# Feed-forward stage of a fused layer gradient in column blocks of 768 and 512 with one buffer of row tiles, and zero fills moved among the stages

## The chip, the cores and the metric

The kernel runs on one core of one Trainium2 chip. The metric is the device time of one launch in microseconds; the kernel before has a median of 601.91 us over three runs (601.8 to 602.16). Engines are named as in the profile: PE (matmul), DVE (vector), ACT (scalar), POOL and SP (here issuers of DMA above all). Queue q0 carries the DMAs that POOL issues, q1 those that SP issues; both run on the same 16 DMA engines.

## The reference, cut to what matters

One token goes through a conditioned layer: modulation of `c` by `w_mod`, attention of 32 heads over the last 4096 keys of a cache, and a gated feed-forward stage. The outputs are the layer's value and the gradient of every input for a given `grad_out`.

```python
mod = silu(c) @ w_mod                       # sa, ca, ga, sb, cb, gb
h = layernorm(x) * (1 + ca) + sa
x = x + ga * attention(h, k_cache[-4096:], v_cache[-4096:], wq, wo)
h = layernorm(x) * (1 + cb) + sb
g = h @ w_gate ; u = h @ w_up               # 1024 -> 3584
x = x + gb * ((sigmoid(g) * u) @ w_down)    # 3584 -> 1024
# and jax.vjp of all of it: 10 gradients
```

The gradients of the two caches are 65536 rows per head group, zero except for the last 4096. The kernel writes those zeros itself: 120 pieces of 1 MB (six of them 960 KB), called fills, which make up about half of the 246.54 MB that the DMA engines move.

## The kernel before, in words

The order of all work is written out by hand (`manual_schedule`): each engine runs its instructions in the order of the source. DMA goes mostly through POOL's queue: `zero(n)` pops and issues n fills there, `load_ug` (L942) loads row tiles of `w_up` and `w_gate`, and gradient tiles are stored there. SP's queue carries `w_down` (`load_wd`, L931), small pieces of `w_mod` and some stores at the end. A fill has no data to wait for. With `after=` it waits for a named instruction (`dep`), so that it starts at a chosen point of the computation, and it stands in POOL's order like everything else. A DMA on POOL's queue also waits until the one eight places ahead of it on that queue has landed.

The stage that the change rewrites treats the 3584 hidden columns in NB = 7 blocks of FB = 512. For a block q:

- `load_ug(q, j0, 4)` brings four of the eight row tiles j of `w_up` (k = 0) or `w_gate` (k = 1), 128 x 4 x 512, 512 KB each. The tiles have two buffers (`q % 2` in `ug_v`), so those of block q + 2 are loaded while block q + 1 is worked on.
- `front(q)` (L1030): 32 matmuls give h @ w_up and h @ w_gate of the block as rows in a PSUM bank (`fg`).
- `gates` (L1039 on): DVE turns the rows into columns (a multiply by a mask and a sum), ACT takes sigmoid, and writes zeros into the bank for the next block.
- `turned` (L1053, L1054): the first JT = 3 row tiles are transposed on PE and copied back by ACT, so that PE can do their part of dh2 in `turned_mm` (L1060). The other five are done by DVE.
- `wd_ttr` (L253 through `ttr`): four sums over rows of `w_down` times a broadcast gradient (`b1k`), which give dhh.
- `hh_ops`, `ffn_mm` (L1073): the hidden values and their product with `w_down`, 32 matmuls of one column. After each half, `load_wd` reloads the two rows of the tile just used for the next block: 512 KB on SP's queue.
- `dug_part` (L1088, L1090): the gradient of g and u is spread over 128 partitions by eight PE transposes; ACT copies one half out, DVE the other.
- Five `ttr` over the remaining row tiles (1024 elements each), in place, give DVE's part of dh2. The loads for block q + 2 and the fills `Z_FFN[q]` are issued between these.

`side(n)` puts n unrelated transposes of `wo` and `v` tiles (L916 on PE, L917 on ACT) between these steps: 46 of them, two at a time. They and `turned` share two PSUM banks. After the stage come the gradient stores: `dwd` (gradient of `w_down`: four outer products on DVE and one 1 MB store), `dw_rows` (gradient of `w_up` and `w_gate`: one 896 KB store per row tile), `dwo`, `sec`, `kv_store` and others, with fills `Z_HAND` and `Z_ROWS` between them. The last statement issues what fills are left.

The two statements that say most about the order in a block, of `turn` and of the loop over q:

```python
gates(); turned(q); side(2); wd_ttr(0); hh_ops(q); first = wd_ttr(1); ffn_mm(q, 0)
side(2); front(q + 1, range(4)); side(2); front(q + 1, range(4, KD))   # then the five ttr of block q
```

Of the kernel before, what the change touches and what calls it, by code (L numbers as in the profile page):

```python
# [22 lines left out]
FB = 512  # L23
NB = F // FB
# [32 lines left out]
Z_FFN = [(1, 0, 1)] + [(1, 1, 1)] * 4 + [(0, 2)]  # L57
Z_HAND = (1, 1, 2, 1, 1)
Z_ROWS = (1, 1, 1, 0, 1, 0, 1, 0)
JT = 3  # L60
JV = KD - JT
@with_exitstack
def kernel(
# [174 lines left out]
    def mulv(out, a, b):  # L238
        return tt(out, a, b, ALU.mult)
# [684 lines left out]
    ug_v = arena[:, 16 * KIB:48 * KIB].rearrange("p (h q j k f) -> p q h j k f", h=2, q=2, j=4, k=2)  # L924
    wd_v = ar(152, 8).rearrange("p (i d) -> p i d", i=4)

    def wd_dram(t, q):
        return t[q * FB:(q + 1) * FB, :].rearrange("(p i) d -> p i d", i=4)

    def load_wd(q, i0=0, n=4):  # L930
        nc.sync.dma_start(out=wd_v[:, i0:i0 + n, :], in_=wd_dram(B_w_down, q)[:, i0:i0 + n, :])  # L931

    def ug_part(view, q, j0, n):
        return view[:, j0:j0 + n, q * FB:(q + 1) * FB]

    def ug_tile(q, k, j0, n):
        return ug_v[:, q % 2, j0 // 4, j0 % 4:j0 % 4 + n, k, :]
# [26 lines left out]
    load_ug(0, 0, 4, (0,))  # L964
    fold_T[2]()
    bch(1)
    load_ug(0, 0, 4, (1,))
    fold_T[3]()
    bch(1)
    load_ug(0, 4, 4, (0,))  # L970
    bch(1)
    load_ug(0, 4, 4, (1,))
# [4 lines left out]
    load_wd(0, 0, 2)  # L977
# [3 lines left out]
    B_t[4] = scr  # L981
    mod_tiles(md_ps, sb_t, range(4, 8), False)
# [13 lines left out]
    load_ug(1, 0, 4)  # L996
    tr_unit(B_t[6], ar(60, 2))()
    load_wd(0, 2, 2)
# [4 lines left out]
    load_ug(1, 4, 4)  # L1003
# [11 lines left out]
    dug_b = scr  # L1015
    dug_b2 = dug_b.rearrange("p (k f) -> p k f", k=2)
    dh2acc = vt([P, NB * JV], "dh2acc")
    small = {k: vt([P, 4], k, dt) for k, dt in
             (("sg", FP32), ("om", FP32), ("dhh", FP32), ("hh_bf", BF16), ("hom", FP32))}
    hh_all = vt([P, 4 * NB], "hh_all")  # L1020
    dug_all = rows_all[:, 64:64 + 8 * NB]
    fg = new_bank("fg")
    nc.vector.memset(fg, 0.0)
    gu_ps, ffn_ps, dh2_ps = fg[:, 0:256], fg[:, 256:256 + KD], fg[:, 272:272 + JT]
    ffn = vt([P, KD], "ffn")
    gu_t = gb_rest
# [6 lines left out]
    def front(q, js=range(KD)):  # L1033
        for j in js:
            w = ug_v[:, q % 2, j // 4, j % 4, :, :].rearrange("p k (r i) -> p k i r", i=4)
            ffn_rows(gu_ps, h2_bf[:, j:j + 1], w, j == KD - 1)

    def gates():
        rows_to_cols(gu_t, gu_ps, 8, gu_ps)  # L1039
        nc.scalar.activation(out=small["sg"], in_=gu_t[:, 4:8], func=ACT.Sigmoid)  # L1040
        nc.scalar.activation(out=small["om"], in_=gu_t[:, 4:8], func=ACT.Sigmoid, scale=-1.0)
        nc.scalar.activation(out=gu_ps.rearrange("p (n d) -> p n d", n=2), func=ACT.Copy, scale=0.0,
                             in_=ident_f.rearrange("p (n d) -> p n d", n=1).broadcast_to([P, 2, P]))

    def ug_flat(q, j):
        return ug_v[:, q % 2, j // 4, j % 4, :, :].rearrange("p k f -> p (k f)")

    def turned(q):
        for j in range(JT):
            w, tp = ug_flat(q, j), new_tp("tp_ug")  # L1050
            for b in range(8):
                k, i = divmod(b, 4)
                nc.tensor.transpose(tp[:, b * P:(b + 1) * P], w[:, k * FB + i:k * FB + i + FB - 3:4], ident_bf[:, :])  # L1053
            nc.scalar.copy(out=w, in_=tp[:, :])  # L1054

    def turned_mm(q):
        for j in range(JT):
            w = ug_flat(q, j)
            for b in range(8):
                nc.tensor.matmul(dh2_ps[:, j:j + 1], lhsT=w[:, b * P:(b + 1) * P],  # L1060
                                 rhs=dug_all[:, 8 * q + b:8 * q + b + 1], start=False,
                                 stop=(q == NB - 1 and b == 7), skip_group_check=True)

    def hh_ops(q):
        hh, up = hh_all[:, 4 * q:4 * q + 4], gu_t[:, 0:4]
        mulv(small["hh_bf"], small["sg"], up)
        mulv(hh, small["sg"], up)
        mulv(small["hom"], hh, small["om"])

    def ffn_mm(q, i0):  # L1070
        for i in (i0, i0 + 1):
            for k in range(KD):
                nc.tensor.matmul(ffn_ps[:, k:k + 1], lhsT=wd_v[:, i, k * P:(k + 1) * P],  # L1073
                                 rhs=small["hh_bf"][:, i:i + 1], start=False,
                                 stop=(q == NB - 1 and i == 3), skip_group_check=True)

    def wd_ttr(*rows):
        for i in rows:
            last = ttr(scr, wd_v[:, i, :], b1k, small["dhh"][:, i:i + 1])
        return last  # L1080

    def dug_part(q):
        dug = dug_all[:, 8 * q:8 * q + 8]
        mulv(dug[:, 0:4], small["dhh"], small["sg"])
        mulv(dug[:, 4:8], small["dhh"], small["hom"])
        tp = new_tp("tp_dug")
        for i in range(8):
            nc.tensor.transpose(tp[:, i * P:(i + 1) * P], dug[:, i:i + 1].broadcast_to([P, P]), ident_bf[:, :])  # L1088
        o, v = dug_b.rearrange("p (k f i) -> p k f i", k=2, i=4), tp.rearrange("p (k i f) -> p k f i", k=2, i=4)
        nc.scalar.copy(out=o[:, 0, :, :], in_=v[:, 0, :, :])  # L1090
        return cp(o[:, 1, :, :], v[:, 1, :, :])

    dug_row = [ar(o, 7) for o in (24, 152)]
    def dug_rows(k):
        for q0 in range(0, NB, 2):
            n = min(2, NB - q0)
            tp = new_tp("tp_rows")
            for b in range(4 * n):
                c0 = 8 * (q0 + b // 4) + 4 * k + b % 4
                nc.tensor.transpose(tp[:, b * P:(b + 1) * P], dug_all[:, c0:c0 + 1].broadcast_to([P, P]), ident_bf[:, :])  # L1100
            nc.scalar.copy(out=dug_row[k][:, q0 * FB:(q0 + n) * FB].rearrange("p (s f j) -> p s f j", f=P, j=4),
                           in_=tp[:, 0:n * FB].rearrange("p (s j f) -> p s f j", f=P, j=4))

# [5 lines left out]
    def dwd(q, off, outer):  # L1109
        t = ar(off, 8).rearrange("p (i d) -> p i d", i=4)  # L1110
        for i in range(4):
            outer(t[:, i, :], hh_all[:, 4 * q + i:4 * q + i + 1], b1k)

        def store():
            nc.gpsimd.dma_start(out=wd_dram(out_8, q), in_=t)
        return store
# [7 lines left out]
    def turn(q, fills=0):  # L1124
        gates()
        turned(q)
        side(2)
        wd_ttr(0)
        hh_ops(q)
        first = wd_ttr(1)  # L1130
        ffn_mm(q, 0)
        if q + 1 < NB:
            load_wd(q + 1, 0, 2)
        zero(fills, wd_ttr(2, 3))
        ffn_mm(q, 2)
        if q + 1 < NB:
            load_wd(q + 1, 2, 2)
        last = dug_part(q)
        turned_mm(q)
        return first, last  # L1140

    rot[:] = [(psum, "mm"), (prq, "rq")]
    side(2)
    front(0)
    zero(Z_FOLD[2])
    zero(Z_FOLD[3], turn(0)[0])
    for q in range(NB):
        more = q + 1 < NB
        if more:
            side(2)  # L1150
            front(q + 1, range(4))
            side(2)
            front(q + 1, range(4, KD))
        else:
            side(len(jobs))
        for j in range(JT, KD):
            w = ug_flat(q, j)
            ttr(w, w, dug_b, dh2acc[:, q * JV + j - JT:q * JV + j - JT + 1])
            if j == 3:
                if q + 2 < NB:  # L1160
                    load_ug(q + 2, 0, 4, (0,))
                    zero(Z_FFN[q][0])
                    load_ug(q + 2, 0, 4, (1,))
                elif more:
                    zero(Z_FFN[q][1])
                    dwd(0, 24, outer_dve)()
                    zero(Z_HAND[0])
                else:
                    dwd(3, 16, outer_dve)()
                    zero(Z_HAND[3])  # L1170
        if q + 2 < NB:
            load_ug(q + 2, 4, 4, (0,))
            zero(Z_FFN[q][1])
            load_ug(q + 2, 4, 4, (1,))
            turn(q + 1, Z_FFN[q][2])
        elif more:
            dwd(1, 40, outer_dve)()
            zero(Z_HAND[1])
            turn(q + 1)
            dwd(2, 152, outer_dve)()  # L1180
            zero(Z_HAND[2])
            dug_rows(0)
    dwd(4, 32, outer_dve)()
    zero(Z_HAND[4])
# [16 lines left out]
    dx1b, m2 = layernorm_bwd_col(dln2, ln2, rstd2, "ln2b", lambda: dwd(5, 152, outer_dve)())  # L1201
# [6 lines left out]
    zero(Z_ROWS[0])  # L1208
    bcast(dattn_bf, KD, dattn_b, "V")
# [88 lines left out]
    for b in range(2):  # L1298
# [7 lines left out]
        for hh in range(4):  # L1306
            nc.tensor.matmul(dov[:, b, :, hh], lhsT=do_sb[:, hh * P:(hh + 1) * P], rhs=ident_bf[:, 0::32],
                             start=True, stop=True)
    for g in range(G):
        tr_unit(N_sb[:, g * 1024:(g + 1) * 1024])()  # L1310
    dwd(6, 32, outer_dve)()
    dw_rows(0, 2, 40, outer_dve)
    zero(Z_ROWS[1])
    dwo(2)
    dwo(0)
    do_bf = vt([P, HQ], "do_bf", BF16)
    cp(do_bf, do_ps)
    dwo(4)
# [178 lines left out]
```

## Time and profile before

| what | value |
|---|---|
| median of 3 runs | 601.91 us |
| time of the profiled execution | 602.02 us |
| its span, first to last instruction | 600.2 us |
| DMA moved | 246.54 MB, mean 411 GB/s; q0 93.8%, q1 9.5% of 16 engines' span |
| busy: PE, DVE, ACT, POOL | 415.4 (69%), 353.8 (59%), 247.5 (41%), 148.0 (25%) us |
| granted TensorE clock, mean | 0.808 |
| feed-forward stage, first `front` to the last block's sums | about 311.7 to 430 us of the span |
| packets under 8 KB | 18864 of 33645 |

Times in the trace count from the span's start. 1.8 us of the profiled execution lie outside its span. "DMA share" is the sum of the packets' own durations over 16 engines' time: it passes 1 where packets of two queues overlap on an engine, so the GB/s beside it say better whether the engines are at work.

### The profile page before, as it was taken

What the parts mean: (1) busy time and instruction counts of PE and PEld (TensorE: products, weight loads), DVE (VectorE), ACT (ScalarE), POOL (GpSimd) and SP (SyncE); (2) the same over time, 40 slices, a digit from 0 to 9 for tenths busy, and PEclk for the clock granted to TensorE, in tenths of its full rate; (3) what the DMA queues carried; (4) which work ended last, traced back from release to release, by engine and by line L of the source; (5) the groups of instructions that cost most, each with busy time, mean ns of one, the idle gap of its engine ahead of it and who ended that gap; (6) DMA issues with size and microseconds to landing.
All of it is one profiled execution on the core that took longest, in us unless ns stands there. A gap on an engine that the chain in (4) does not pass through costs nothing.

```text
span 600.2 us, 9825 instructions
## 1 busy us (share of the span) xinstructions
PE 415.4 (69%) x4004; PEld 246.7 (41%) x4004; DVE 353.8 (59%) x647; ACT 247.5 (41%) x398; POOL 148.0 (25%) x249
## 2 busy tenths in 40 slices
PE   3996789999999999979776477766652056364300
PEld 2784434334345455435455465555532045131000
DVE  3755499999510030194738488878877056876800
ACT  2489515558211024112246366665632057373200
POOL 3113113212222122222223033241335133241100
PEclk9998699999999999998988578787676557555555
DMA  8999999999999999999999999999999999999997
GB/s 349 421 418 423 411 457 406 430 424 438 433 420 391 453 433 393 461 425 412 387 417 417 347 355 408 409 409 421 424 425 425 429 396 425 423 425 419 419 415 235
DMA packets 33645, 246.54 MB, mean 411 GB/s; under 512 B 4781, under 2 KB 4781, under 8 KB 18864
## 3 DMA queue, kind: packets, MB, share of 16 engines
q0 software_dynamic: 28320, 225.98, 93.8%
q1 hardware_dynamic: 5232, 19.93, 9.5%
q8 instruction: 31, 0.51, 0.3%
q14 instruction: 14, 0.11, 0.1%
q10 hardware_dynamic: 48, 0.01, 0.0%
HBM read 78.13 MB, written 185.60 MB: 439 GB/s over the span
## 4 chain that ended last, share of the span: by engine, by line
PE 37%; DMA 21%; DVE 20%; ACT 8%; issue 7%; POOL 3%; ACTq 0%; POOLq 0%; DVEq 0%; SPq 0%
PE b_ps L773 17%; DMA out_dram<-arena 12%; DVE arena L236 6%; PE n_ps L716 6%; DMA arena<-in_B_w_down_dram 5%; DVE arena L249 4%; DVE arena L253 3%; ACT arena L527 2%; ACT arena L1281 2%; PE t_ps L674 2%; DMA out_dram<-zeros 2%; DVE scr L253 2%; DMA arena<-in_B_w_gate_dram 1%; PE tp_k L506 1%; PE tp_side L916 1%
## 5 line engine op out<-in xcount | busy, mean ns | idle before, releaser
L773 PE MATMUL b_ps<-arena 128*128 128x512 bf16 x512 | 118.6, 384 | 1.1 <-ACT arena L917 1.1
L917 ACT COPY arena<-tp_side 128x1024 bf16<-128x1024 bf16 x62 | 60.8, 1018 | 50.5 <-PE tp_side L916 50.3
L236 DVE TENSOR_TENSOR arena<-arena 128x2048 bf16<-128x2048 bf16 x64 | 76.5, 1223 | 2.3 <-PE n_ps L716 0.3
L773 PEld LDWEIGHTS <-arena 128*128 128x128 bf16 x512 | 49.3, 99 | 58.9 <-issue 5.8
L716 PE MATMUL n_ps<-arena 128*128 128x512 bf16 x256 | 65.6, 378 | 5.8 <-DVE arena L236 4.2
L203 POOL DMA_DIRECT2D out_dram<-out_dram x68 | 33.7, 496 | 116.8 <-PE n_ps L716 38.4
L916 PE MATMUL tp_side<-ident_bf,arena 128*128 128x128 bf16 x496 | 48.2, 262 | 12.7 <-DVE arena L236 4.7
L916 PEld LDWEIGHTS <-arena 128*128 128x128 bf16 x496 | 40.3, 120 | 22.1 <-issue 13.6
L249 DVE TENSOR_SCALAR arena<-arena,h 128x3584 bf16<-128x3584 bf16 (+1 forms) x24 | 28.6, 1192 | 32.1 <-DMA out_dram<-arena 32.1
L209 POOL DMA_DIRECT2D out_dram<-zeros x46 | 25.9, 566 | 67.6 <-DVE rows_all L236 23.0
L716 PEld LDWEIGHTS <-arena 128*128 128x128 bf16 x256 | 24.6, 97 | 41.2 <-issue 15.8
L253 DVE CUSTOM_DVE_ANT_0 arena<-arena,scr 128x1024 bf16<-128x1024 bf16 x35 | 40.8, 1220 | 0.2
L1277 PE MATMUL ps_kv<-arena 32*128 32x512 bf16 x64 | 24.2, 588 | 22.6 <-DVE arena L257 12.8
L253 DVE CUSTOM_DVE_ANT_0 scr<-arena,b1k 128x1024 bf16<-128x1024 bf16 x28 | 34.2, 1223 | 7.5 <-DMA arena<-in_B_w_down_dram 7.0
L1281 ACT ACTIVATE arena<-ps_kv 128x512 bf16<-128x512 f32 x48 | 25.4, 690 | 31.3 <-PE ps_kv L1277 31.1
L676 ACT CAST arena<-t_ps 128x512 bf16<-128x512 f32 x56 | 30.1, 589 | 12.1 <-PE t_ps L674 12.1
L245 DVE CAST arena<-b_ps 128x512 bf16<-128x512 f32 x6 | 4.2, 692 | 50.8 <-PE b_ps L773 50.8
L1053 PE MATMUL tp_ug<-ident_bf,arena 128*128 128x128 bf16 x168 | 14.4, 244 | 17.7 <-ACT arena L1054 17.7
L527 ACT COPY arena<-tp_wq 128x1024 bf16<-128x1024 bf16 x23 | 21.4, 1066 | 7.3 <-PE tp_wq L525 7.3
L1277 PEld LDWEIGHTS <-arena 32*128 32x128 bf16 x64 | 6.9, 117 | 38.7 <-issue 37.8
L1341 PE MATMUL dh_ps<-dattn_bf,arena 128*128 128x1 bf16 x48 | 2.1, 167 | 29.2 <-ACT arena L1337 29.2
L942 POOL DMA_DIRECT2D arena<-in_B_w_up_dram x14 | 10.7, 761 | 43.1 <-DVE dh2acc L253 22.7
(325 smaller groups left out, 686.8 us busy)
## 6 DMA issues: line engine op xcount, KB each, us to landing
out_dram<-zeros POOLq DMA_DIRECT2D x46, 1024.0 KB, 11.8
out_dram<-arena POOLq DMA_DIRECT2D x35, 1024.0 KB, 11.8
out_dram<-arena POOLq DMA_DIRECT2D x16, 896.0 KB, 11.5
arena<-in_A_wq_dram POOLq DMA_DIRECT2D x8, 1024.0 KB, 21.1
arena<-in_A_wo_dram POOLq DMA_DIRECT2D x8, 1024.0 KB, 12.5
arena<-in_w_mod_dram POOLq DMA_DIRECT2D x7, 1024.0 KB, 18.7
arena<-in_B_w_up_dram POOLq DMA_DIRECT2D x14, 512.0 KB, 9.4
arena<-in_B_w_gate_dram POOLq DMA_DIRECT2D x14, 512.0 KB, 13.3
```

Of the source, the lines that this page charges most:

```text
L203: ins = nc.gpsimd.dma_start(out=as_rows(region, BIGP).bitcast(FP32), in_=zero_src[:, 0:P * ZW // 4].rearrange("i (p x) -> (i p) x", p=BIGP ...
L236: return nc.vector.tensor_tensor(out=out, in0=a, in1=b, op=op)
L249: return nc.vector.tensor_scalar(out=out, in0=a, scalar1=s1, scalar2=None, op0=op0)
L253: return nc.vector.tensor_tensor_reduce(out=out, in0=w, in1=b, scale=1.0, scalar=0.0, op0=ALU.mult, op1=ALU.add, accum_out=acc)
L527: nc.scalar.copy(out=blk, in_=tp[:, :])
L676: nc.scalar.copy(out=o, in_=ps)
L716: mm = nc.tensor.matmul(nbank[k][:, :], lhsT=k_nat[:, g, t_ * DH:(t_ + 1) * DH], rhs=vp[:, t_ % 2, 4 * k:4 * k + 4, :].rearrange("p h d -> ...
L773: mm = nc.tensor.matmul(bbank[p][k][:, :], lhsT=a4[:, p, h, :], rhs=wo_t[u][:, a, k * 512:(k + 1) * 512], start=(i == 0 and a == 0), stop= ...
L916: nc.tensor.transpose(tp[:, i * P:(i + 1) * P], blk[:, i * P:(i + 1) * P], ident_bf[:, :])
L917: nc.scalar.copy(out=blk if dst is None else dst, in_=tp[:, :])
L1277: nc.tensor.matmul(ps[:, :], lhsT=rows[r, t8 * P:(t8 + 1) * P], rhs=bd[r, :], start=True, stop=True, tile_position=(32 * tc_, 0))
L1281: nc.scalar.activation(out=o, in_=v, func=ACT.Copy, scale=float(scale))
```

## The change

The blocks become five: `NI = (6, 6, 6, 6, 4)` groups of 128 columns, so four blocks of 768 columns and one of 512. There is one buffer of row tiles (24 KB instead of 32 KB per partition). A pair of row tiles of the next block is loaded as soon as this block has done with the old ones: j = 0, 1 after `turned_mm`, then 2 and 3, 4 and 5, 6 and 7 after their `ug_ttr`. A load is 128 x 2 x 768 (384 KB). JT falls from 3 to 2, so DVE does six tiles of 1536 elements instead of five of 1024.

The sums over the first n - 1 rows of `w_down` (`wd_ttr`) stand ahead of `gates` in DVE's order, only the last one behind. `w_down` comes as six row tiles, the first four in one 1 MB load, the other two in a 512 KB load. `dug_part` goes through two PSUM tiles and a buffer of its own (`dug_b`, no more `scr`). DVE's copy of the second half waits for PE there, where it waited for ACT.

Per block of the loop POOL issues one fill after `dug_part`, eight loads, and three fills behind the last pair (`Z_FFN = [(1, 0, 0, 3)] * 4`). The fills of the stage up to `Z_HAND` stay 22. `Z_ROWS` becomes eight ones (it had five), and the last statement finds none left, where it issued three. `dwd` stores come in parts of three rows (768 KB), nine in all instead of seven of 1 MB.

```diff
-FB = 512
-NB = F // FB
+NI = (6, 6, 6, 6, 4)
+NB = len(NI)
+I0 = [sum(NI[0:q]) for q in range(NB)]
+KF = F // P
...
-Z_FFN = [(1, 0, 1)] + [(1, 1, 1)] * 4 + [(0, 2)]
-Z_HAND = (1, 1, 2, 1, 1)
-Z_ROWS = (1, 1, 1, 0, 1, 0, 1, 0)
-JT = 3
+Z_FFN = [(1, 0, 0, 3)] * 4
+Z_HAND = (2, 2, 2)
+Z_ROWS = (1, 1, 1, 1, 1, 1, 1, 1)
+JT = 2
...
+    wd_off = [152, 154, 156, 158, 44, 46]
+    wd_row = [ar(o, 2) for o in wd_off]
+    dug_b = ar(40, 3)
...
+    def ug_off(q, j):
+        if NI[q] == 6:
+            return 16 + 3 * j
+        return 16 + 2 * j if j < 4 else 24 + 2 * j
...
-    load_ug(0, 0, 4, (0,))
+    load_ug(0, 0, 2, (0,))
...
-    load_ug(0, 4, 4, (0,))
+    load_ug(0, 6, 2, (0,))
...
-    load_ug(1, 0, 4)
+    load_ug(0, 2, 2)
...
-    load_ug(1, 4, 4)
+    load_ug(0, 4, 2)
...
     side(2)
-    front(0)
+    front(0, (0, 1, 6, 7))
+    turned(0)
     zero(Z_FOLD[2])
-    zero(Z_FOLD[3], turn(0)[0])
+    front(0, range(2, 6))
+    zero(Z_FOLD[3], wd_ttr(*range(NI[0] - 1)))
     for q in range(NB):
...
+        gates(q)
+        wd_ttr(n - 1)
+        side(1)
+        hh_ops(q)
+        dug_cols(q)
+        last = dug_part(q)
+        zero(z[0] if more else Z_HAND[0], last)
+        turned_mm(q)
+        if more:
+            load_ug(q + 1, 0, 2)
+        ffn_mm(q, range(4))
+        if more:
+            load_wd(q + 1, 0, 4)
+        ffn_mm(q, range(4, n))
+        if more and NI[q + 1] > 4:
+            load_wd(q + 1, 4, 2)
+        side(4)
...
+        ug_ttr(q, 2)
+        ug_ttr(q, 3)
+        if more and NI[q + 1] == 6:
+            load_ug(q + 1, 2, 2)
+            zero(z[1])
...
+        ug_ttr(q, 4)
+        ug_ttr(q, 5)
+        if more:
+            load_ug(q + 1, 4 if NI[q + 1] == 6 else 2, 2)
+            zero(z[2])
...
+        ug_ttr(q, 6)
+        ug_ttr(q, 7)
+        if more:
+            if NI[q + 1] == 6:
+                load_ug(q + 1, 6, 2)
+            else:
+                load_ug(q + 1, 4, 4)
+                dwd(24)
+            zero(z[3])
+            front(q + 1, (0, 1))
+            turned(q + 1)
+            side(2)
+            front(q + 1, (2, 3))
+            side(1)
+            front(q + 1, (4, 5))
+            side(1)
+            front(q + 1, (6, 7))
+            wd_ttr(*range(NI[q + 1] - 1))
```

The old `turn` and the old loop body are gone. In the rest of the diff `front`, `gates`, `turned`, `turned_mm`, `hh_ops`, `dug_rows` and `dwd` take the block's width, and five more `dwd` calls stand among the gradient stores.

## Prediction

> **What bounds the kernel now.** I read the page's slices first, then the windows over the feed-forward stage, then the chain and the DMA issues there.
>
> ```profile
> DMA  8999999999999999999999999999999999999997
> GB/s 349 421 418 423 411 457 406 430 424 438 433 420 391 453 433 393 461 425 412 387 417 417 347 355 408 409 409 421 424 425 425 429 396 425 423 425 419 419 415 235
> ```
>
> The DMA engines are the bound almost everywhere. No other engine passes 69% of the span. So an edit is worth what it adds to or takes from the time in which the 16 engines have nothing to move, plus any change in what moving costs. Two slices are low inside the span, 22 and 23 (330 to 360 us), and they lie in the stage that is rewritten. Its windows (columns: length, busy time of PE, PEld, DVE, ACT, POOL, clock, DMA share, GB/s):
>
> ```profile
> 326.00:337.00 11.00, 4.60 (x72) 3.46 (x61) 5.45 (x13) 6.41 (x10) 1.65 (x3) 0.78 1.10 410
> 337.00:350.00 13.00, 8.26 (x128) 6.33 (x129) 9.59 (x19) 4.49 (x5) 2.71 (x5) 0.66 0.87 290
> 364.00:378.00 14.00, 10.40 (x160) 8.35 (x160) 12.14 (x27) 9.90 (x13) 4.64 (x7) 0.76 1.10 403
> 394.00:410.00 16.00, 12.60 (x200) 9.74 (x193) 13.46 (x29) 9.71 (x13) 5.14 (x9) 0.80 1.14 410
> 410.00:430.00 20.00, 13.26 (x165) 11.96 (x163) 18.04 (x39) 13.78 (x18) 3.69 (x7) 0.66 1.12 424
> ```
>
> Full engines move 410 GB/s of the stage's mix and 424 of stores and fills alone. Six windows (311.7, 327.9, 349.5, 364.1, 378.5, 395 to 410.7, each from one `gates` to the next but the first) give 407, 336, 402, 405, 410, 411: over 99 us a mean of 391.6. Against 410 that is 99 x 18.4 / 410 = 4.4 us lost, nearly all at 337 to 350. Why, the chain says:
>
> ```profile
> 318.64 1.22 DVE scr L253
> 319.90 0.04 issue
> 319.94 18.48 DMA arena<-in_B_w_down_dram
> ...
> 341.31 1.05 PE tp_dug L1088 x8
> ...
> 343.05 0.70 DVE scr L245
> ```
>
> `w_down` of block 1, asked for at 319.07 and 319.94, came at 338.4; behind it stood POOL's next fill, issued at 341.35 (it waits for `dug_part`'s products), and the loads behind that. The queue ran dry at 337. From 350 on, two buffers of row tiles keep loads issued a block ahead: `gates` follow each other by 14.6 us (349.5, 364.1, 378.5), a block moves 6.29 MB = 15.3 us at 410, so the engines always have work.
>
> **What the change removes.** With another order that dry spell has no reason to recur as such: -4.4 us. What is late next is the question.
>
> **A block of 768 after the change.** It moves 4 fills (4.19 MB), row tiles 3.15 and `w_down` 1.57 MB: 8.91 MB, 21.7 us at 410. Its clock starts at DVE's `gates`, t. Rows: multiply plus sum 0.81 us (364.08 to 364.89) x 1.5 = 1.2; one row sum 1.15 (period in a run of `ttr`); five small products 0.6; so dug at t+3.0. PE's twelve transposes: eight took 0.62 to 1.05, so 1.2: t+4.2. DVE's copy 0.69 x 1.5 = 1.0: t+5.2, where the fill is issued, then the pair 0, 1, which also waits for `turned_mm` (24 in 0.8 us, t+5.0). `w_down` is issued after 32 more matmuls (1.0): t+6.0. At 341.35 a fill went into an empty queue and the rate stayed at 210 until 344: about 2.5 us to the stream; SP's should take 1 to 2.5. Bytes flow from t+7.
>
> DVE then does six sums of 1536: 1.147 x 1.5 = 1.7 each, to t+15.4, and issues follow them: pair 2, 3 at t+8.7, pair 4, 5 at t+12, pair 6, 7 with three fills behind it at t+15.4. Five sums over `w_down` (1.27 apart) end at t+21.8.
>
> The long chain is PE's. `front(q+1, (0, 1))` stands ahead of everything else and needs pair 0, 1. Ahead of that pair, or beside it, the engines move the fill (1.05 MB) and all of `w_down` (1.57): 3.41 MB with the pair, 8.3 us, so it lands at t+15.3 to 16.5; I take 15.6 for 16 engines that don't end together. Before, the same tiles had landed a block earlier. Behind it: `front` of two tiles 0.8 (16 matmuls of 256 took 1.08); `turned`, 0.5 and four ACT copies of 768 (1.02 x 0.75 = 0.8) through two PSUM banks, 3.7; the second unit of `side` 0.7; then three `front` of 0.8 and two `side` units of 0.7 to 1.0 between: 9.4 us, bounds 8.8 (all transposes 0.61 per eight) and 10.4 (all 1.01). The next `gates` come at t+25.0 (23.8 to 26.5), against t+21.8 for DVE and t+21.7 for the bytes. Three fills behind the last pair last 7.7 us and are gone when `gates` begin or soon after, and new bytes flow only at t+7: 3.3 us of dry queue per block.
>
> The row of 14.6 us beside that: x 1.5 is 21.9, so DVE alone would keep pace. The single buffer loses it.
>
> **The first block.** Its later pairs are issued where block 1's loads stood:
>
> ```profile
> arena<-in_B_w_up_dram POOLq DMA_DIRECT2D x1, 512.0 KB, 18.8
> arena<-in_B_w_gate_dram POOLq DMA_DIRECT2D x1, 512.0 KB, 15.9
> ```
>
> These two (window 302 to 307, issued at 302.13 and 306.38; last column: us to landing) land at 320.9 and 322.3. With 0.9 MB less ahead of the pair 4, 5 it lands near 320, and `gates(0)` go from 313.7 to t = 321. The queue: before, without what was issued at 324 to 329 (3.15 MB), it would have been empty at 337.5 - 7.7 = 329.8; now 1.05 MB fewer row tiles and 0.52 MB less `w_down` stand in it, 3.8 us: dry at 326.0, bytes again at 328: 2.0 us. Blocks 1, 2, 3 start at 346, 371, 396, with 3.3 us each. In block 3 the next block's tiles are smaller: 8.13 MB, 19.8 us, but its last loads wait for the sixth sum and land near t+20, `gates(4)` at t+22: 2.0 us, and 0.7 more until `Z_HAND`'s fills. Sum 2.0 + 9.9 + 2.0 + 0.7 = 14.6 us dry.
>
> [...] In the window 319 to 325 only q0 moves (113.2% share) although `w_down` had been asked for at 319; in 374 to 381 q1 has 43.9% beside q0's 66.3%. [...]
>
> **Small terms.** Row tiles come in packets of 3 KB per partition instead of 4, `w_down` in larger ones: blocks whose half is 4 KB packets run at 410 against 424, 0.5 us per 3.15 MB; a third more packets add 0 to 0.7 us over the 12.6 MB: +0.5. Seven turns become five and ACT copies fewer turned tiles, while DVE takes six tiles of eight: nothing either way, since DVE's 21.8 lies under the 25.0; without that cover it would be 0.1 us over the bytes' 21.7 per block. The three last fills move into `Z_ROWS`: the engines are full there (422 to 430), so the bytes only change places. At the end SP's queue alone moved 397 GB/s (568 to 573, q1 96.4%) against 424, and without POOL's three fills its last 3 MB run alone: +0.5. They may fill the dips at 480 to 500 (393, 417): 0 to -0.9, I take -0.4. Sum +0.6. `dwd` in nine parts: same bytes, 0.
>
> **The forecast.** On the profiled execution's 602.0 (1.8 of it outside the span): -4.4 + 14.6 + 0.6 = 612.8, and 0.1 less against the median 601.91: 612.7. A period of 24.5, nearer the chain's lower bound, gives 1.5 less; I set 612.0.
>
> **Rivals.**
> First, slower by less (0.22): `w_down` waits behind POOL's work, as at 319 to 325. Then pair 0, 1 lands after 1.84 MB, at t+12.2, PE is ready at t+21.6, and the last pair's landing decides, about t+22.7: 1.0 us dry per block. 2.0 + 3.0 + 2.0 + 0.7 = 7.7: 602.0 - 4.4 + 7.7 + 0.6 = 605.9. For it: 18.48 us of waiting in the chain. Against: in the later blocks `w_down` landed in about 10.
>
> Second, faster (0.24): the queue never runs dry, because sums ahead of `gates` and three fills behind the last pair cover the turn. It decides at a period of 21.7: if PE's chain behind pair 0, 1 were 6 us, or the pair landed by t+12 and the last `front` within 0.3 of the last pair. Price: 602.0 - 4.4 + 0.6 = 598.2, up to 601 with the first block's 2.0 and a little at each turn. For it: from 364 to 378 ACT is busy for 9.90 of 14 us and PE for 10.40, so both have room. Against: 8.3 us of bytes ahead of the pair.
>
> Third, slower still: all PE steps at the slow rate, period 26.0, 3 us more, 615.8. Row: the clock was 0.50 at 340 to 344, and eight transposes took 1.01 against 0.61. [...] I give it 0.12 beside 0.35 for the forecast's own period, and 0.02 to worse.
>
> That the order isn't as written is no rival: the built program has five sums ahead of the multiply on DVE and one and three fills around eight loads on POOL. No change within 0.2% (1.2 us, about what a measurement of this kernel can tell): 0.05, a dry time that happens to equal the old one.
>
> Faster 0.24, same 0.05, slower 0.71. The range of 8 in 10 reaches from the faster case, 598.0, to 617.0, the slow period with its first block late; the likeliest case alone is 607 to 617.
>
> **What would show it.** Right: `gates` 24 to 26 us apart; PE waiting for pair 0, 1 each time; GB/s dips of 3 us at each turn; the gradient stages unchanged at 420 to 430. Wrong: turns at 22 us, or 410 GB/s through 320 to 430.

## The result, and the profile after

The changed kernel takes 617.03 us (median of 4 runs, 615.8 to 617.65), the kernel before 601.86 in the same comparison: a ratio of 1.0258 (1.0228 to 1.0288). It is slower, as forecast, but by 15.2 us where the forecast of 612.0 said 10.1 (its sum, 612.7, said 10.8), and 0.03 us beyond the top of the range. The profiled execution took 615.8 us, its span is 613.8, 13.6 more than before. (Runs of the kernel before lie in two groups some 2 us apart, so below, differences under 2 us are not read from times alone.)

The slices of the page, where only 22 and 23 had been low:

```profile
DMA  9999999999999999999999997989999999999997
GB/s 352 421 417 422 414 462 403 400 459 428 392 455 426 431 427 421 415 437 412 427 395 374 341 316 274 376 295 316 424 424 411 424 427 423 425 425 426 424 419 306
```

Slices 21 to 27 (322 to 430 us) are now low, the whole feed-forward stage, and what follows is at 411 to 427 up to the last slice. The windows from each `gates` to the next (same columns as before the change; the last figure is GB/s, and the one ahead of it the DMA share, which passes 1 with one queue alone as well: 1.13 from 319 to 325 in the kernel before, where only q0 moved):

```profile
321.30:348.80 27.50, 17.37 (x214) 11.86 (x213) 19.90 (x32) 13.24 (x17) 8.63 (x13) 0.63 1.05 387
348.80:376.80 28.00, 16.48 (x214) 11.03 (x215) 19.92 (x32) 13.18 (x17) 7.96 (x12) 0.70 0.91 325
376.80:403.60 26.80, 16.70 (x214) 11.36 (x214) 19.93 (x32) 13.24 (x17) 7.88 (x12) 0.75 0.86 316
403.60:427.70 24.10, 14.78 (x207) 11.56 (x207) 18.82 (x32) 12.05 (x17) 7.87 (x12) 0.72 0.78 271
427.70:440.00 12.30, 8.81 (x126) 7.81 (x125) 11.33 (x27) 8.73 (x12) 3.54 (x7) 0.72 1.13 421
```

Against 410 GB/s that is 27.5 x 23 / 410 = 1.5 us lost in the first block, then 5.8, 6.1 and 8.2: 21.6 us, where the stage lost 4.4 before. No compute engine is near full in them (DVE 19.9 of 28.0, PE 16.5). So what ends each block is a wait. The chain through the first turn, from one block to the next (start, length, what; steps under 0.2 us are left out):

```profile
328.18 10.21 DMA arena<-in_B_w_gate_dram
338.44 1.19 PE fg L1040 x8
339.63 0.79 PE tp_ug L1071 x6
340.48 0.81 ACT arena L1072
341.33 0.77 PE tp_ug L1071 x6
342.18 0.41 ACT arena L1072
342.58 0.29 issue
342.87 0.81 ACT arena L1072
343.73 0.61 PE tp_side L918 x8
344.34 1.12 PE fg L1040 x8
345.45 0.55 PE tp_side L918 x8
346.01 1.12 PE fg L1040 x8
347.12 0.55 PE tp_side L918 x8
347.68 1.15 PE fg L1040 x8
348.85 0.58 DVE fg L238
```

This is the forecast's long chain, piece for piece: the gate half of pair 0, 1 asked for at 328.18 and in use at 338.44; two tiles of `front`; the turning, PE and ACT in turn; three more `front` with `side` units between; then `gates`. The block began at 321.27, so the period, the time from one block's `gates` to the next, is 27.6 us. The list of waits in that stage has one line for all turns, the first block's last pair and the last block's pairs among them (total, times, longest):

```profile
PE fg L1040 <- DMA arena<-in_B_w_gate_dram: 31.4, 6, 8.1
```

And the second turn seen from the DMA engines, in slices of 0.7 us from 349 to 377:

```profile
DMA  9940000059399999999999999999999999999999
GB/s 386 375 141 12 0 0 0 0 47 140 117 421 410 421 410 445 398 380 408 415 408 390 389 386 375 362 380 375 369 367 390 453 448 424 410 410 445 421 433 433
```

The last fill's bytes end at 351; the next block's first loads and fill are issued at 354.1, and the rate is full from 357 on: some 3.5 us of next to nothing and two of little. Where only row tiles move (364 to 370), the rate is 362 to 390, not 410.

The fourth block is another case. Its chain runs through DVE's sums to the last load, issued at 420.07 and landed 5.67 us later.

### The profile page after: what moved, and what is told of

It is laid out like the page before. It is cut to its first block, busy times and chain, and to the rows that moved or that the text cites. A ratio compares the mean times of both kernels' runs of the same rounds, so it can differ in the third digit from the quotient of the medians.

```text
span 613.8 us, 9435 instructions
## 1 busy us (share of the span) xinstructions
PE 413.4 (67%) x3803; PEld 236.4 (39%) x3828; DVE 359.3 (59%) x621; ACT 241.3 (39%) x390; POOL 155.4 (25%) x261
## 2 busy tenths in 40 slices
DMA packets 33517, 246.53 MB, mean 402 GB/s; under 512 B 4910, under 2 KB 5422, under 8 KB 18993
## 4 chain that ended last, share of the span: by engine, by line
PE 37%; DMA 24%; DVE 19%; issue 9%; ACT 6%; POOL 2%; ACTq 0%; DVEq 0%; POOLq 0%
PE b_ps L775 14%; DMA out_dram<-arena 13%; DMA arena<-in_B_w_gate_dram 8%; DVE arena L238 6%; PE n_ps L718 6%; DVE arena L251 5%; PE fg L1040 3%; DMA arena<-in_w_mod_dram 2%; DVE arena L255 2%; ACT arena L529 2%; PE t_ps L676 2%; PE w_ps L471 1%; ACT arena L1072 1%; PE tp_k L508 1%; PE tp_side L918 1%
## 5 line engine op out<-in xcount | busy, mean ns | idle before, releaser
L775 PE MATMUL b_ps<-arena 128*128 128x512 bf16 x494 | 114.3, 379 | 2.4 <-ACT arena L919 1.1
L775 PEld LDWEIGHTS <-arena 128*128 128x128 bf16 x512 | 48.7, 98 | 57.5 <-issue 3.4
L255 DVE CUSTOM_DVE_ANT_0 arena<-arena 128x1536 bf16<-128x1536 bf16 (+1 forms) x38 | 57.5, 1558 | 0.7
L918 PE MATMUL tp_side<-ident_bf,arena 128*128 128x128 bf16 x496 | 47.6, 258 | 11.4 <-DVE arena L238 6.2
L211 POOL DMA_DIRECT2D out_dram<-zeros x46 | 26.2, 572 | 101.3 <-DVE arena L247 57.1
L918 PEld LDWEIGHTS <-arena 128*128 128x128 bf16 x496 | 39.4, 118 | 29.1 <-issue 18.8
L1317 PE MATMUL ps_kv<-arena 32*128 32x512 bf16 x64 | 24.4, 588 | 28.8 <-DVE arena L259 15.8
L1040 PE MATMUL fg<-arena,h_bf 128*32 128x384 bf16 (+1 forms) x160 | 21.3, 623 | 31.5 <-DMA arena<-in_B_w_gate_dram 31.4
L718 PEld LDWEIGHTS <-arena 128*128 128x128 bf16 x256 | 24.6, 97 | 41.3 <-issue 15.8
L1321 ACT ACTIVATE arena<-ps_kv 128x512 bf16<-128x512 f32 x48 | 25.4, 698 | 37.5 <-PE ps_kv L1317 37.3
L1072 ACT COPY arena<-tp_ug 128x768 bf16<-128x768 bf16 (+1 forms) x20 | 14.1, 762 | 31.4 <-PE tp_ug L1071 31.3
L953 POOL DMA_DIRECT2D arena<-in_B_w_up_dram x19 | 13.9, 730 | 31.1 <-DVE dh2acc L255 23.0
```

Source lines behind the costliest of these rows:

```text
L255: return nc.vector.tensor_tensor_reduce(out=out, in0=w, in1=b, scale=1.0, scalar=0.0, op0=ALU.mult, op1=ALU.add, accum_out=acc)
L718: mm = nc.tensor.matmul(nbank[k][:, :], lhsT=k_nat[:, g, t_ * DH:(t_ + 1) * DH], rhs=vp[:, t_ % 2, 4 * k:4 * k + 4, :].rearrange("p h d -> ...
L775: mm = nc.tensor.matmul(bbank[p][k][:, :], lhsT=a4[:, p, h, :], rhs=wo_t[u][:, a, k * 512:(k + 1) * 512], start=(i == 0 and a == 0), stop= ...
L918: nc.tensor.transpose(tp[:, i * P:(i + 1) * P], blk[:, i * P:(i + 1) * P], ident_bf[:, :])
L1040: nc.tensor.matmul(out[32 * a:32 * a + 32, :], lhsT=col.broadcast_to([P, 32]), rhs=w[..., 32 * a:32 * a + 32], start=False, stop=stop, til ...
L1317: nc.tensor.matmul(ps[:, :], lhsT=rows[r, t8 * P:(t8 + 1) * P], rhs=bd[r, :], start=True, stop=True, tile_position=(32 * tc_, 0))
```

## The experiments

All but those named as the kernel before are the changed kernel with one edit, or with the edits that are named. Differences are against its 617.03 us; t is the start of a block's `gates`, as in the prediction.

**The first fill behind the first pair.** In the block's body, `zero(z[0])` goes from ahead of `turned_mm(q)` to behind the first load:

```diff
-        zero(z[0] if more else Z_HAND[0], last)
         turned_mm(q)
         if more:
             load_ug(q + 1, 0, 2)
+        zero(z[0] if more else Z_HAND[0], last)
```

> The changed kernel with one edit: a block's first fill of 1 MB goes into POOL's queue behind the gate and up loads of the next block's first two row tiles, no longer ahead of them. Bytes and work are unchanged. Theory (the turn from one block to the next waits for that pair of row tiles, which comes behind the fill and next to 1.5 MB of w_down, and the matmul chain of some 10.3 us runs only behind it): the pair lands some 2.5 us earlier, the periods between gates go from 27.6, 28.0, 26.8 to about 25, so about 609 to 610. Rival (only the sum of the bytes in the queue counts, so what stands first in it changes nothing): 616 to 617.5.

607.43 us (606.98 to 608.02), 9.6 less; ratio to before 1.012 (1.0089 to 1.015). It is more than was expected, because the pair came 3.5 to 4.2 us earlier and not 2.5: it landed at t+13.6, 13.6 and 13.0 instead of 17.1, 17.8 and 16.5, and the periods went from 27.6, 28.0, 26.8 to 24.3, 25.4, 24.3. The same bytes in another order: the theory holds, the rival (only their sum counts) does not. What is late next is the last pair, by the chain of that run:

```profile
335.14 1.67 DVE arena L255
337.12 0.71 POOL arena L953
337.83 6.35 DMA arena<-in_B_w_gate_dram
344.31 1.22 PE fg L1040 x8
345.56 0.58 DVE fg L238
```

DVE's sums release the last loads at 337.1, the second of them lands 6.35 us behind its issue, and one `front` stands behind it.

**`w_down` held back.** Its two loads depend on the first sum over the row tiles:

```diff
-        if more:
-            load_wd(q + 1, 0, 4)
...
-        ug_ttr(q, 2)
+        first = ug_ttr(q, 2)
+        if more:
+            dep(load_wd(q + 1, 0, 4), first)
```

> The changed kernel with one edit: the next block's w_down (1 MB and 512 KB) is issued only when the first of VectorE's six sums over the row tiles is done, so that it doesn't share the DMA engines with the first fill and the first pair of row tiles. Theory (as told for the fill put behind): 1.5 MB less in front of the first pair, which takes 3.5 us off it; the pair lands at about 13 to 14 us behind the gates instead of 17, the periods are about 24 to 25, so about 606 to 609. Rival (w_down takes the pair's place as the last that the next block waits for, or the bytes count in whatever order): the last pair or w_down's last rows end a period of 27 to 28, 615 to 618.

613.44 us (612.27 to 614.16), 3.6 less. `w_down` was issued only 0.9 to 1.7 us later (t+7.3 instead of 5.8 in the first block), so the edit did less than meant: the pair landed at t+15.6, 15.6 and 15.3, not 13 to 14, and the chain behind it took 11.4 and 11.5 us at the first two turns instead of 10.4 and 10.2 (sixteen `side` transposes 1.87 us instead of 1.31; the granted clock was 0.62 over each of these two blocks, 0.63 and 0.70 in the changed kernel). In kind it agrees with the theory; its number was missed.

**The chain made short.** `front(q + 1, range(KD))`, then `turned(q + 1)`, with all eight `side` units where four stood, ahead of PE's wait for the pair.

> The changed kernel with one edit: the next block's eight row tiles go through the forward matmuls in order, and the turning of the first two row tiles, with the side units between, stands behind them and ahead of nothing that loads (the side units stand in front of the loads instead). Theory (period = landing of the first pair + the chain of matmuls, copies and side units behind it, 10.3 us): the chain behind the first pair shrinks to about 4.6 us, but the last pair lands 6.3 us behind the first, so that 1 to 1.2 us of matmuls behind the last pair end the period: about 24.5 to 26, so about 608 to 612. Rival (the DMA queue alone ends the period, because its dry stretch is set by when the loads may be issued): the time stays at 616 to 618.

614.18 us (613.44 to 616.03), 2.9 less, with periods 24.4, 27.0, 26.1 and 26.2. Neither number came. The first turn did what the theory said (24.4); the others paid elsewhere (two stretches of that run's chain):

```profile
347.75 0.66 ACT arena L1072
348.50 0.65 issue
349.15 0.21 ACT sg L1055
...
363.62 7.78 DMA arena<-in_B_w_gate_dram
371.54 1.19 PE fg L1040 x8
```

ACT's copies of the turned tiles now stand ahead of the sigmoid that the products of `gates` need. The block's first fill is issued at t+6.9 and 7.0 instead of 5.2 and 5.6, and the last pair, which now ends the period, is late by that.

**The fills of the last stage as before.** `Z_ROWS = (1, 1, 1, 0, 1, 0, 1, 0)`.

> The changed kernel with one edit: the fills of the last stage are placed as before the change (three of the eight slots are empty and their fills come at the very end). Theory (spreading the fills costs nothing and brings nothing where the DMA engines are busy anyhow; the loss is in the feed-forward blocks): 616 to 618. Rival (the fills put in earlier push back stores that the end waits for, which is where the time beyond the forecast went): about 612.

619.93 us (618.77 to 622.19), 2.9 more, with `gates` at the same times as in the changed kernel to 0.5 us. Neither side had this: spreading the fills is a gain, and it hid part of the loss in the blocks.

**A fill in the dry time.** `Z_FFN = [(1, 0, 0, 4)] * 3 + [(1, 0, 0, 3)]`, `Z_HAND = (1, 1, 1)`.

> The changed kernel with one more 1 MB fill behind the last pair of row tiles in each of the first three blocks (Z_FFN's last number 4 in place of 3), taken from the hand-over behind the last block (Z_HAND 1, 1, 1 in place of 2, 2, 2). Theory (the time lost is DMA engines that stand idle at each turn, from the end of the fills 3 us behind the gates to the first new bytes at about 7 us, while the next block can't load before its predecessor's sums are done): a fill of 2.45 us fits into the idle 4 us and delays nothing, so gates come at the same times as in the changed kernel, with 3 MB more done: 7.3 us less, 609 to 611. Rival (the queue is not idle but waits on something that the fill only prolongs, so that each turn comes later by about as much as the fill takes): 616 to 618.

612.63 us (611.29 to 614.56), 4.4 less where 7.3 were expected. The hand-over, with three fills fewer, ran at 347 GB/s from 429.7 to 440 instead of 421: 10.3 x 74 / 421 = 1.8 us. And the second period was 29.5 instead of 28.0, so `gates(4)` came 2.0 us later. It is not shown that the fill did this. The pair landed only 0.3 us later (t+18.1), while the chain behind it took 11.4 us instead of 10.2, with the granted clock at 0.50 from 366.5 to 371; and the last run below, whose blocks are those of the changed kernel without any fill added, had the same second period (29.6). The dry time is real; a fill put in it is worth its 2.45 us (in the changed kernel, fills behind each other landed 2.4 us apart, at 375.3, 377.7 and 380.1) less what it leaves empty elsewhere.

**Both.** The fill behind the pair, `Z_FFN = [(1, 0, 0, 4)] * 2 + [(1, 0, 0, 5), (1, 0, 1, 3)]`, `Z_HAND = (1, 1, 1)`, `Z_ROWS = (0, 0, 1, 1, 1, 1, 1, 1)`.

> The changed kernel with the first fill of a block behind the first pair of row tiles, and five more fills in the blocks: Z_FFN (1,0,0,4), (1,0,0,4), (1,0,0,5), (1,0,1,3), taken from the hand-over (Z_HAND 1, 1, 1) and from the first two slots of the stage behind it. With the fill put behind alone it was 607.4, and its windows between gates moved 377, 367, 362 and 313 GB/s. Theory (idle DMA engines are the loss, and both remedies add up as far as idle time is left): some 2 us for each of the first two turns, 3 at the third and 1 to 1.5 in the fourth block, so 598 to 601, below the kernel before. Rival (with the fill put behind, the last pair ends the period, so every further fill ahead of the next block's loads delays the turn by its own 2.4 us): 606 to 609.

602.82 us (601.61 to 605.37, 10 runs), ratio to before 1.0038 (1.0019 to 1.0056). Its windows:

```profile
321.50:345.80 24.30, 17.80 (x214) 12.30 (x214) 19.93 (x32) 13.23 (x17) 9.23 (x14) 0.62 1.09 385
345.80:372.20 26.40, 16.45 (x215) 10.88 (x216) 19.95 (x33) 13.16 (x17) 8.54 (x13) 0.74 1.14 402
372.20:397.00 24.80, 16.22 (x214) 10.85 (x213) 19.92 (x32) 13.22 (x17) 9.88 (x15) 0.79 1.15 393
397.00:423.00 26.00, 15.13 (x206) 11.71 (x207) 18.81 (x32) 12.02 (x17) 7.69 (x12) 0.71 1.11 413
423.00:440.00 17.00, 11.01 (x148) 9.33 (x146) 14.77 (x33) 12.10 (x17) 3.40 (x6) 0.70 1.00 376
```

The four blocks lose 1.5, 0.5, 1.0 and nothing. `gates(4)` come only 4.7 us earlier than in the changed kernel, but 14.2 us are back: most of them from work done in time that had been idle. What kept it from the 598 to 601 expected is the emptied places: 376 GB/s at the hand-over in the last row, and 412 from 440 to 520, where the changed kernel had 422.

**The kernel before, its dry spell filled.** `Z_FOLD = (1, 1, 1, 0)`, first entry of `Z_FFN` `(1, 2, 1)`.

> The kernel before with its own dry stretch filled: two fills go from ahead of the gates of the first block (Z_FOLD's last number 0 in place of 2) into its second half (Z_FFN's first entry (1, 2, 1) in place of (1, 0, 1)), so that POOL's queue holds work while the DMA engines stand idle behind the second block's w_down; same bytes. Theory (the 4.4 us that the kernel before loses in this stage are one dry stretch, and any transfer put there is worth its length): the stage loses up to 4.4 us less, 597 to 599. Rival (the two fills only swap places with the loads they now stand ahead of, so that the next gates come later and the dry stretch moves on): 600.5 to 602.

598.85 us (598.3 to 600.17), ratio 0.9973 (0.9957 to 0.999). The third `gates` came at 343.7 instead of 349.5, and 328 to 344 moved 413 GB/s. As the theory said.

**The kernel before, with the last stage's fills spread and nothing else.** `Z_ROWS` all 1.

> The kernel before with only the last part of the change: one fill in each of the eight slots of the last stage, none left for the very end (Z_ROWS all 1). In the changed kernel, undoing this cost 2.9 us. Theory (without fills between them, the last stores don't keep the DMA engines full; that depends on how far the engines are behind the last work, and the kernel before is ahead by some 15 us of queue): the kernel before has no such loss, its last 40 us moved 423 and 409 to 425 GB/s, so 601 to 602. Rival (the spread fills are worth the same in both kernels): 598.5 to 599.5.

594.11 us (594.06 to 597.01), ratio 0.99 (0.9867 to 0.9933); its profiled span is 595.2, 5.0 below. More than even the rival had. Of the 5.0, 3.0 lie behind the last landing: it came 4.3 us ahead of the end before and 1.3 here. The other 2.0 are earlier bytes, 480 to 520 at 424 GB/s instead of 414 among them.

**Columns read in order.** In `front`, `(k r i) -> p k i r` becomes `(k i r) -> p k i r`.

> The changed kernel with one edit: the forward matmuls over w_gate and w_up read 32 neighbouring columns at a time, no longer every sixth one. It leaves out the right assignment of columns to rows, so what it computes behind that is not the reference's; loads, bytes and the number of matmuls are the same. Theory (a matmul of 384 columns took 0.14 us, one of 256 columns 0.067 us at the same granted clock, because the price goes by the stretch of memory that is stepped over, 12 bytes a step in place of 8): the eight of two row tiles take 0.8 us or less in place of 1.19, the chain behind the first pair goes from 10.3 to 8.7 us, the periods from 27.5 to about 26, so 612 to 613. Rival (the price goes by the columns or by the number of matmuls): they stay at 1.19 us, and the time at 616 to 618.

612.04 us (610.9 to 613.12), 5.0 less, as the theory had it. The matmuls (PE's timeline), first and second pair of a block and one pair of the last block, which has 256 columns, and below them two lines of the changed kernel:

```profile
338.40 0.83 PE L1040 MATMUL fg<-arena,h_bf 128*32 128x384 bf16 x8 [7.42 <-DMA arena<-in_B_w_gate_dram]
...
343.91 0.51 PE L1040 MATMUL fg<-arena,h_bf 128*32 128x384 bf16 x8
...
422.53 0.40 PE L1040 MATMUL fg<-arena,h_bf 128*32 128x256 bf16 x8 [1.39 <-DMA arena<-in_B_w_gate_dram]
```

```profile
344.27 1.19 PE L1040 MATMUL fg<-arena,h_bf 128*32 128x384 bf16 x8
...
425.88 0.62 PE L1040 MATMUL fg<-arena,h_bf 128*32 128x256 bf16 x8 [1.14 <-DMA arena<-in_B_w_gate_dram]
```

In order, 0.83 us at a granted clock of 0.50 and 0.51 at 1.00; with 12 bytes a step 1.19 at either (0.50 at 338.4, 1.00 at 344.3); with 8 bytes a step, for two thirds of the columns, 0.63 at 0.50 (at 418.6) and 0.62 at 1.00, against 0.40 in order at 1.00. The chain behind the pair took 8.1 us at the first turn and 9.6 at the second, for 10.4 and 10.2. So the step is the price of `front`.

**TensorE kept busy.** 64 transposes of `ident_bf` behind `side(4)`.

> The changed kernel with 64 more transposes of a constant tile on TensorE in each of the first four blocks, behind the side units and ahead of the wait for the next block's first pair, where TensorE idles 7 to 8 us; nobody reads them. Theory (the chain behind the pair is slow by the granted clock, 0.5 for most of each wait: six transposes took 0.79 us, sixteen of a side unit 1.87 or 1.31): with the clock kept up the chain takes 8.8 to 9.3 us in place of 10.3, and the time falls by 3 to 4.5 us, 612.5 to 614. Rival (the chain is copies and matmuls whose price the clock doesn't move, 1.19 us for the eight forward matmuls at 0.5 and at 1.0 alike): 616 to 618, or later by up to 3 us a turn where the added work runs past the pair's landing.

616.25 us (613.65 to 617.09): no difference that can be read, and the chain at the first turn took the same 10.4 us. This run leaves the clock's share open: granted 1.00 up to 338, the clock was at 0.57 from 338 to 342, with PE idle for 2.3 us before the pair came.

**Both edits of the kernel before together.**

> The kernel before with both edits that were tried on it alone: its dry stretch filled (598.85 for 601.44) and a fill in each slot of the last stage (594.11). Theory (the first takes idle time out of the feed-forward stage, the second the wait at the end for POOL's queue to drain, so they add up): 2.5 to 3.5 us below the second alone, 590.5 to 592. Rival (both use the same fills, and what the first gains is lost as a gap in the last stage): 594 to 596.

594.19 us (593.74 to 595.13), ratio 0.9894 (0.9867 to 0.9922): the rival's number. Beside the spread fills, filling the dry spell brought nothing measurable here; its window from 314 to 330 fell to 364 GB/s, so the dry time had moved ahead. These two kernels, with the spread fills alone or with both edits, beat the kernel before and after.

**What the end waits for.** Three runs. First the last four stores with their queues swapped: `kv_store(out_2, dk_home, g, tail if g < 2 else nc.gpsimd)`.

> The changed kernel with one edit at its end: of the last four stores of 1 MB, SP's queue takes the first two and POOL's queue the last two, in place of the other way round; bytes and order of the work are the same. Theory (the end waits for POOL's drain, which ended 2.7 to 3.5 us behind the landing of the last transfer of POOL's own queue in eight profiles, and the part of the change that leaves no fill for the very end is worth what it takes out of this wait): the last landing stays near 612.8 in the profile, now POOL's, and the span grows by 2 to 2.7 us, so 619 to 620. Rival (undoing the spread fills cost 2.9 us because the queue ran thin, not for the drain): the time stays at 616 to 618.

616.91 us (616.88 to 617.54), the rival's number, but the premise failed: SP's stores still landed last (613.7, POOL's 610.5). Then one fill at the end, `Z_ROWS = (1, 1, 1, 1, 1, 1, 1, 0)`:

> The changed kernel with one fill of 1 MB, not three, left for the very end (the last of the eight slots empty). Theory (the end waits for POOL's drain, 2.75 us behind the last landing in POOL's queue, so it matters whether POOL's or SP's transfers land last and not how many fills are late): one fill behind the last stores makes POOL's queue the last, at about 613 in the profile, and costs nearly what three cost, 2 to 2.9 us: 619 to 620. Rival (the last stores run thin for want of fills between them, each worth a third of 2.9 us): 617.5 to 618.2.

616.0 us (615.87 to 617.07), the premise again unmet (613.9 and 610.5). Then all four stores on POOL's queue, no fill at the end:

> The changed kernel with the last two stores of 1 MB on POOL's queue too, where SP's queue had them; all fills stay spread, bytes and work are the same. In the two runs before this one SP's stores still landed last (613.7 and 613.9, POOL's at 610.5), so that POOL's drain was hidden. Theory (the end is the later of SP's last landing and POOL's last landing plus 2.75 us): with 2 MB more on POOL's queue and 2 MB less on SP's, POOL's transfers land last, at about 612.5 to 613.5, and the drain shows: 2 to 2.7 us more, 618.5 to 620. Rival (it is the fills at the very end themselves that cost, whoever lands last): 615.5 to 617.5.

619.08 us (618.88 to 620.36), ratio to before 1.0316 (1.0286 to 1.0345): 2.05 more, with POOL's last landing at 613.5, SP's last packet at 609.1 and the span 617.1. (In this profile `gates(4)` also came 1.5 us later than in the changed kernel's, in blocks that are the same, so the two spans can't be compared as they stand; what can is the time from the last landing to the end, 3.6 us here and 1.1 there.) The final drains, of the changed kernel, of this one and of the kernel before (ns, least, middle and most; start of the first and last):

```profile
L1535 POOLq DRAIN  x3: 51/93/17731, 594.4 to 613.5; - x3
```

```profile
L1535 POOLq DRAIN  x3: 46/102/20016, 596.3 to 616.8; - x3
```

```profile
L1492 POOLq DRAIN  x3: 51/93/29286, 570.2 to 600.0; - x3
```

The long ones end at 594.4 + 17.7 = 612.1, at 616.3 and at 599.5; POOL's own last transfers had landed at 609.4, 613.5 and 595.9. So POOL's drain ends 2.7 to 3.5 us behind its queue's last landing, here and in the other profiles of this case: 2.7 to 2.8 in the changed kernel and its variants, 3.5 in the kernel before and its variants. Where SP's stores land last (the changed kernel, 612.8) it is hidden. Where POOL's do, with three fills or four stores behind all else, the end waits for it. It is not the fill as such: one fill cost nothing.

## Why the prediction was right in sign and short in size

- **The bound and the loss to be removed (-4.4).** Right in kind: the dry spell of the kernel before was one stretch, and two fills put there took 2.6 us off.
- **Where the block starts.** Right. `gates(0)` was forecast for 321 and came at 321.27, the load of pair 4, 5 landing at 320.0 as said; the fill, at t+5.2, was issued at t+5.2 to 5.6.
- **The cause.** Right: each block waits for pair 0, 1, behind the fill and beside `w_down`, then for PE's chain. The fill put behind the pair and the fill in the dry time show it from both sides.
- **The pair's landing: mis-sized.** Forecast t+15.6, measured 17.1, 17.8 and 16.5. At the first turn the queue did not run dry, although the sum said so: two older fills landed only at 327.3 and 329.8, ahead of the new ones. At the second the fill issued at 354.1 sent its first packet at 357.2, 3.1 us later, where bytes were to flow from t+7, 355.8; at the next two turns this took 1.1, and SP's loads took 1.0 to 1.2. And more moved beside the pair than the 3.41 MB of the sum: from the fill's issue to the pair's landing 4.21 MB at the second turn and 3.72 at the third, as the loads of the next pairs were already under way. At 410 GB/s that is 2.0 and 0.8 us, for which the sum had 0.3.
- **The chain behind it: mis-sized.** Forecast 9.4, measured 10.4, 10.2, 10.3. The term is `front`: 0.8 each was 16 matmuls of 256 columns scaled by 1.5; it took 1.12 to 1.19 four times, 1.4 us more in all. At the first turn the turning took 4.1 instead of 3.7, and cheaper `side` units gave 0.8 back.
- **The period, and so the dry time.** 25.0 forecast, 27.6, 28.0 and 26.8 measured. Less the bytes' 21.7 that is 5.9, 6.3 and 5.1 us a turn instead of 3.3; block 3 took 24.0 instead of 22, because its last loads landed at t+22.1, not t+20. By the windows the first block lost 1.5 us where 2.0 were forecast, the next two 5.8 and 6.1 where 3.3 each were, the fourth 8.2 where 6.0 were. Dry and slow 21.6 us instead of 14.6: this is the step that failed, by 7.0. Of it some 0.5 us in the second block is that row tiles alone move slower (an estimate: 7 us at 378 GB/s instead of 410), for which the sum had 0.5 in all.
- **The small terms: wrong sign.** +0.6 was forecast. The three last fills were priced at +0.5 as bytes at the end; taken from there they took 3.2 us off what the end waits for (4.3 behind the last landing before, 1.1 after). The rest of the later stages gave some 0.4, which is what is left over in the sum and is not traced to a place. The packets, for which it had +0.5, were no more in all (33517, against 33645 before). The sum of the profile: 600.2 + 21.6 - 4.4 - 3.2 - 0.4 = 613.8. Two errors of opposite sign made the forecast look closer than its steps were: that is luck.
- **The rivals.** `w_down` behind POOL's work: no, it shared the engines from its first byte, as the sum had it (its first 1 MB landed 7.5 and 8.1 us after issue at the third and fourth turn, the fill beside it 7.5 and 7.6). Why it waited at 319 to 325 in the kernel before stays open. Never dry: no. The slow clock: its time, 615.8, is that of the profiled execution, but not by its cause alone. TensorE idled 6.7 to 8.1 us a turn, and the clock stood at 0.50 when each pair came; it was at 1.00 some 3 us behind it, and the matmuls that were mis-sized took 1.19 us at 0.5 and at 1.0 alike. That the idle time lowers the clock is not shown: at the third turn PE was idle from 386.7, and the clock was 1.00 until 389.6 and 0.50 from 389.8; at the first two it was at 0.50 before the long idle began, with PE busy for 6.1 of the 6.4 us from 352.2 to 358.6. What the clock can cost the transposes shows in the last run above, whose blocks are those of the changed kernel: at its second turn the clock stayed at 0.50 until 375, sixteen `side` transposes took 1.86 us instead of 1.31, the chain 11.5 instead of 10.2, and the period was 29.6.

## What to carry to other kernels

With one buffer, the order of the bytes inside a block can decide when the next one starts, with their number unchanged: put what the next block needs first at the head of the queue, and fills behind it (9.6 us here for one moved line). Where the DMA engines bound a kernel, a slower block can cost next to nothing if its idle time is given work that would have to be done anyway (with both edits the first four blocks still took 24.3 to 26.4 us each, and the kernel 602.82 where the one before took 601.86); but take that work from where it is not needed (the emptied hand-over fell from 421 to 376 GB/s). At the end, let the queue whose completion is cheap land last (here SP's: the end came 1.1 us behind its last landing, and 3.6 behind POOL's when that was last).

## What the runs showed of the hardware that I had not expected

- A matmul's price followed how its moving operand is stepped through. At a granted clock of 1.00, eight matmuls of 384 columns took 1.19 us at 12 bytes a step and 0.51 in order, and eight of 256 columns 0.62 at 8 bytes a step and 0.40 in order.
- POOL's drain ended 2.7 to 3.5 us behind the last landing of its own queue (612.1 for 609.4 in the changed kernel, 599.5 for 595.9 in the kernel before). Where SP's stores landed last, the span ended 1.0 to 1.1 us behind them (612.8 and 613.8 in the changed kernel, 613.7 and 614.7 with the last stores' queues swapped, 613.9 and 615.0 with one fill at the end).
- A POOL transfer into an empty queue sent its first packet 3.1 us after issue at one turn (354.1 to 357.2) and 1.1 at two others (382.4 to 383.5, 409.0 to 410.1), in the same code.
